# Pooled attention with an MLP behind it: one block's sum moves to TensorE, values in one group a head, and new priorities for the planner

## The chip, the cores and the metric

The kernel runs on one core of a Trainium2 chip. The metric is the device time of one launch in microseconds (us), the median of several runs. The engines of the core are TensorE (PE, its weight loads are shown as PEld), VectorE (DVE), ScalarE (ACT), GpSimd (POOL) and SyncE (SP, which only issues transfers here). Each engine works through its own queue in order.

## What is computed

Inputs are q, k, v with 4 batches, 8 heads, 1152 positions and 64 values a head, in float32. Cut to what matters:

```python
q_pool = q.reshape(B, H, S // 2, 2, D).mean(axis=3)        # 576 pooled queries
scores = scale * q_pool @ k.transpose(0, 1, 3, 2)          # 576 x 1152 a head
attn = exp(scores - max(scores))
attn = attn / (sum(attn) + 1e-9)
x = attn @ v                                               # heads side by side: 4 x 576 x 512
h = (x.transpose(0, 2, 1) @ U) @ V
u = x + h.transpose(0, 2, 1)
out = u + relu(u @ w_ch1) @ w_ch2                          # 512 -> 2048 -> 512
```

U, V, w_ch1 and w_ch2 arrive as 64-bit floats and are turned into 32-bit ones on the chip ("decode").

## The kernel before

**A head.** The 1152 keys of a head are nine blocks of 128. Queries and keys are transposed on PE, and split into a high part (rounded) and a low part. PE scans all scores once for the row maxima (lines 643 and 645, into PSUM banks of the class m); DVE reduces each scan to a maximum (line 649). Then PE makes the scores of each block with the maximum already taken off (lines 703 and 704, into banks s), and ACT writes their exponentials to SBUF (line 710). Eight of the nine blocks lie in pairs in seven tiles of a region (p2), the ninth alone in one of two tiles (p1). The sums over keys are made in two steps: an addition of 128 x 576 per block into the tile acc (line 686, seven plus the first, which joins two blocks: eight a head), on DVE or POOL, whichever the planner finds free, and then `total()` (line 721), four matmuls for a pair of heads that add acc over its partitions with a matrix of ones, each on 32 columns of PE, so that four stand side by side. The values (line 729) are matmuls of the exponentials with v, two side by side on 64 columns, into one bank that is copied out by ACT (line 737). After the odd head of a pair the outputs are transposed, divided by the sums and put into X (lines 753 to 780).

**Groups of values.** `GV` (line 267) says in which groups a head's blocks are multiplied with v: in batches 0 and 1 blocks 0 to 5 and then 6 to 8, in batches 2 and 3 all nine at once. In batches 0 and 1 (`APART`) the totals are an operation of their own; in 2 and 3 they follow in the value group of the odd head.

**A batch.** After eight heads `tail` (line 785) makes the low-rank mix and the MLP of the batch; lines 937 and 981 are the first MLP matrix, line 1028 the second. The MLP of a batch runs interleaved with the heads of the next one. The weights are decoded once (lines 409 to 426 and 861, 862, on ACT, DVE and POOL), with the MLP of the first batch, and read back by the later ones. PSUM has three banks of class s and five of class m; value groups, scans, transposes and MLP products all take m.

**What sets the order.** The program doesn't issue in the order of its loops. Each operation goes to a planner (`Plan`, from line 43) with a due time `at`, the engines it may run on, and a cost for each. The planner simulates the five queues with these costs, takes at each step the operation with the earliest due time that can start within 30 ns of the first that can, and fixes the order of every queue and the tile of every buffer. Due times are made of `T(G)`, the start of the head plus G ninths of a head's length (`HEAD0` for the first nine heads, `HEAD` later); SUM, AV, KS, QT, KT, MX0, MXS, MLP_START, MLP_RATE, DEC_START and DEC_LEAD shift single kinds of work. `a_(n)` (line 365) is the planner's cost of an ACT instruction of n elements, MOVE (130 ns) an addition to it for copies between partitions, TSW (300 ns) the planner's cost for a change of PE's column mode. The chip then runs the fixed queues in its own time.

Of the kernel before, what the change touches and what calls it, by code (L numbers as in the profile page):

```python
# [227 lines left out]
def kernel(  # L228
# [17 lines left out]
    nc = tc.nc  # L246
    B, H, S, D = q.shape
    NQ = S // 2
    DM = H * D
    DFF = moe_w_ch1.shape[1]  # L250
    R = moe_U.shape[1]
    U64, V64, W1, W2 = (w.bitcast(I32) for w in (moe_U, moe_V, moe_w_ch1, moe_w_ch2))
    P = 128
    NJ = S // P
    HALF = NQ // 2
# [3 lines left out]
    QP, NQT = 96, 6  # L259
    NG = NJ  # L260
    FG = 2
    QT, KS = -9.70, -11.74
    LEAD = 60e3, 9e3
    WHOLE_KEYS, SPLIT = (False, False, True, True), 8
    NB, QUICK = 320, (False, False, False, True)
    NARROW, NP2 = 256, 7
    GV = [((0, 6), (6, 9))] * 2 + [((0, 9),)] * 2
    TSW = 300.0
    SUM, AV, YT = 0.78, 0.73, 0.79
    NS = 6  # L270
    APART = (True, True, False, False)
    KT, MX0, MXS = 0.77, -8.58, 4.36
    V_LO = slice(2 * R, 3 * R)
    WARM_UP, WARM_N, FILL, FILL_N = 5000.0, 13, 90.0, 70
    NWHOLE = H + 1
    EXP_MIN, EXP_MAX = 2.0 ** -15, 122879.9921875
    SCALE = 0.5 / float(D) ** 0.5
    HEAD0, HEAD = 16.89e3, 21.00e3
    SLOT = HEAD / NG
    MLP_START, MLP_RATE = 4.90, (2.21, 2.21, 2.18, 2.2)  # L280
    DEC_START, DEC_LEAD = 98.0e3, 12.5e3
    SLACK = 30.0
    BIAS, BIAS_FROM = -300.0, 0.0

# [6 lines left out]
    op = plan.op  # L291
# [9 lines left out]
    ones = sb.tile([P, R], F32, name="ones")  # L301
# [7 lines left out]
    def cut(of, first, n, shape, rows=P):  # L309
# [14 lines left out]
        T1=cut(room, 0, 2, (S,)),  # L324
# [5 lines left out]
        acc=slots("acc", 3, [P, NQ]),  # L330
        ay=slots("ay", 2, [P, 2, HALF]),
# [77 lines left out]
    def decode(at, n, load, raw, t, far):  # L409


        tv = lambda: t.t[:, 0:n]
        hi = lambda: raw.t[:, 0:n, 1]
        lo = lambda: raw.t[:, 0:n, 0]
        use = [("raw", "use")]
        for f, nb in load:
            op(at - 5e3, ("sp", dma(nb), f, 0, far, BULK), use + go, [raw])
        op(at, ("act", a_(n), lambda: nc.scalar.activation(tv().bitcast(F32), hi().bitcast(F32), AF.Abs)), [raw] + use, [t])
        op(at, ("act", a_(n), lambda: nc.scalar.activation(lo(), lo().bitcast(U32), AF.Copy, scale=2.0 ** -29)), [raw] + use, [(raw, 1)])
        op(at, ("dve", v2(n), lambda: nc.vector.tensor_scalar(  # L420
            tv().bitcast(F32), tv().bitcast(F32), EXP_MAX, EXP_MIN, op0=ALU.min, op1=ALU.max)), [t], [t], port=True)
        op(at, ("dve", v2(n), lambda: nc.vector.tensor_scalar(
            tv(), tv(), 3, 0x3FFFFFFF, op0=ALU.logical_shift_left, op1=ALU.bitwise_and)), [t], [t], port=True)
        op(at, ("dve", v_(n), lambda: nc.vector.scalar_tensor_tensor(  # L424
            tv(), hi(), -0x40000000, tv(), op0=ALU.bitwise_and, op1=ALU.bitwise_or)), [t, raw] + use, [t], port=True)
        op(at, ("pool", g_(n), lambda: nc.gpsimd.tensor_tensor(tv(), tv(), lo(), op=ALU.add)), [t, (raw, 1)] + use, [t])  # L426
# [71 lines left out]
    def head(n):  # L498
# [7 lines left out]
        T1, T2, T3, Q1, Q2, qb, acc, mp = (new(c) for c in ("T1", "T2", "T3", "Q1", "Q2", "qb", "acc", "mp"))  # L506
        odd = h % 2
        if not odd:
            pair[:] = [new(c) for c in ("ay", "sr", "sm", "rs")] + [[]]
        ay, sr, sm, rs, accs = pair  # L510
        accs.append(acc)
        op(T(-17), ("sp", dma(294912), lambda: nc.sync.dma_start(
            qt.t, q[b, h].rearrange("(t p r) d -> p t (r d)", p=QP, r=2)), 0, 1500, BULK), go if n > 1 else [], [qt])
        op(T(KS - 1), dual(NQT * D, lambda e: e.tensor_tensor(
# [47 lines left out]
        def turn_whole(part, j0, j1):  # L562

            pt_ = new("m", KEEP[1])
            n2, n1 = (j1 - j0 + 1) // 2 * P, (j1 - j0) // 2 * P
            kt_blocks = range(j0, j1, 2)

            def kT():
                for i, j in enumerate(kt_blocks):
                    m = 2 if j + 1 < j1 else 1  # L570
                    nc.tensor.transpose(pt_.t[0:m * D, i * P:(i + 1) * P], kt.t[:, j:j + m].rearrange("p a d -> p (a d)"), ident)

            at = T(QT + KT * (1 + part))
            op(at, ("pe", len(kt_blocks) * TP, kT), [(kt, 0), (T1, "use")], [pt_])
            at += 0.6 * (T(1) - T(0))
            halves = (slice(0, D), slice(D, P))
            here = lambda z: T1.t[:, j0 * P:j1 * P].rearrange("p (j i) -> p j i", i=P)[:, z::2]
            there = lambda z: pt_.t[halves[z], 0:(n1 if z else n2)].rearrange("p (j i) -> p j i", i=P)
            for z, n_ in enumerate((n2, n1)):
                if n_: op(at, ("act", a_(n_, True), lambda z=z: nc.scalar.activation(here(z)[halves[z]], there(z), AF.Copy)), [pt_], [(T1, part, z)])  # L580
            for z, n_ in enumerate((n2, n1)):
                if n_: op(at, ("dve", v_(n_) + 90, lambda z=z: nc.vector.tensor_tensor(  # L582
                    here(z)[halves[1 - z]], there(z), here(z)[halves[z]].bitcast(F32), op=ALU.subtract)),
                   [pt_, (T1, part, z)], [(T1, part, 2 + z)])
            for z, n_ in enumerate((n2, n1)):
                if n_:
                    op(at + 0.8 * (T(1) - T(0)), ("act", a_(n_, True) + z * MOVE, lambda z=z: nc.scalar.activation(
                        T2.t[0:D, j0 * P:j1 * P].rearrange("p (j i) -> p j i", i=P)[:, z::2], there(z), AF.Copy)), [pt_], [(T2, part, z)])
            c0 = j0 // 2 * P
            if part == 0:  # L590
                op(at, ("act", a_(n2, True), lambda: nc.scalar.activation(T3.t[:, c0:c0 + n2], pt_.t[:, 0:n2], AF.Copy)), [pt_], [(T3, 0)])
            else:
                if n1: op(at, ("act", a_(n1, True), lambda: nc.scalar.activation(T3.t[:, c0:c0 + n1], pt_.t[:, 0:n1], AF.Copy)), [pt_], [(T3, 1)])
                for z in range(2):
                    op(at, ("act", a_(D, True) + z * MOVE, lambda z=z: nc.scalar.activation(
                        T3.t[halves[z], c0 + n1:], pt_.t[0:D, n1 + z * D:n1 + (z + 1) * D], AF.Copy)), [pt_], [(T3, 2 + z)])
            return [(T1, part, i) for i in range(4)]

# [10 lines left out]
        else:  # L609
# [13 lines left out]
            que, way = (nc.scalar, lambda f, nbytes, far: ("act", 500, f, far)) if n else (  # L623
                nc.sync, lambda f, nbytes, far: ("sp", dma(nbytes), f, 175, 800))
            for z in range(2):
                op(T(-7), ("act", a_(S // 2) + z * MOVE, lambda z=z: nc.scalar.activation(
                    T3.t[z * 64:z * 64 + 64], T1.t[0:D, z * S // 2:(z + 1) * S // 2].bitcast(F32), AF.Copy)),
                   t1[0:2] if z == 0 else t1[1:], [(T3, z)])
            op(T(-6 if n else -20), way(lambda: que.dma_start(T2.t[0:D].bitcast(F32), T1.t[0:D].bitcast(F32)), 294912, 3300), t1, [(T2, p_, z) for p_ in range(2) for z in range(2)])
# [58 lines left out]
        for j in range(NJ):  # L688
            if j % 2 == 0:
# [7 lines left out]
                for js, qa, qz, when in todo:  # L697
                    ss, nq = new("s"), qz - qa

                    def score(js=js, qa=qa, qz=qz, nq=nq, ss=ss):  # L700
# [9 lines left out]
                    op(T(when + 0.1), ("act", a_(len(js) * nq, True), lambda js=js, qa=qa, qz=qz, nq=nq, ss=ss, p=pu[j], e=js[0] % 2: nc.scalar.activation(  # L710
                        p.t[:, e:e + len(js), qa:qz], ss.t[:, 0:len(js) * nq].rearrange("p (a n) -> p a n", n=nq), AF.Exp, scale=SCALE)),
                       [ss], [(pu[j], i % 2, 1 if qa else 0) for i in js])
            if j > 0:
                add(T(j + SUM), unit(0) if j == 1 else (lambda: acc.t), unit(j), keys((0, 1)) if j == 1 else keys((j,)) + [acc])

        pa, pk = new("m"), new("m") if odd else None

        def total():
            for e, hf in ((e, hf) for hf in range(2) for e in range(2)):
                g = 32 * (2 * hf + e)  # L720
                nc.tensor.matmul(pk.t[g:g + 32, 0:HALF], ones, accs[e].t[:, hf * HALF:(hf + 1) * HALF], start=True, stop=True)  # L721

        for j0, j1 in GV[b]:
            last = j1 == NJ and odd and not APART[b]

            def value(js=range(j0, j1), last=last):
                for j in js:
                    for hf in range(2):
                        nc.tensor.matmul(pa.t[hf * D:(hf + 1) * D, 0:HALF], vt.t[:, j], pu[j].t[:, j % 2, hf * HALF:(hf + 1) * HALF],  # L729
                                         start=(j == 0), stop=(j == NJ - 1))  # L730
                if last:
                    total()

            n_ = j1 - j0 + last
            op(T(j1 - 0.5 + AV), ("pe", n_ * 4 * (HALF / 2.4 + 2.0) + TSW, value),
               [(vt, 0)] + keys(range(j0, j1)) + (accs if last else []), [pa] + ([pk] if last else []))
        op(T(NJ + AV), ("act", a_(HALF, True), lambda: nc.scalar.activation(ay.t[:, odd], pa.t[:, 0:HALF], AF.Copy)), [pa], [(ay, odd)])

        if not odd:
            return  # L740
        if APART[b]:
            op(T(NJ + AV), ("pe", 4 * (HALF / 2.4 + 2.0) + TSW, total), accs, [pk])
        op(T(NJ + AV), ("act", a_(HALF, True), lambda: nc.scalar.activation(sr.t, pk.t[:, 0:HALF], AF.Copy)), [pk], [sr])

        first = (0, P, HALF - P)
# [39 lines left out]
    def tail(b, clock):  # L785
# [29 lines left out]
                now += mm(DM)  # L815
        trow, z = new("tr"), new("xs")
        tr, ts = (lambda: trow.t), (lambda: z.t[:, 0])
        op(now, ("act", a_(DM, True), lambda: nc.scalar.activation(tr()[0:R], ptm.t[0:R], AF.Copy)), [ptm], [(trow, 0)])
        op(now, ("act", a_(DM, True), lambda: nc.scalar.activation(tr()[3 * R:4 * R], ptm.t[R:2 * R], AF.Copy)), [ptm], [(trow, 3)])
        for c in range(1, 3):  # L820
            op(now, ("sp", dma(65536), lambda c=c: nc.sync.dma_start(tr()[c * R:(c + 1) * R], tr()[0:R]), 175), [(trow, 0)], [(trow, c)])
        op(now, ("act", a_(DM), lambda: nc.scalar.activation(ts(), tr(), AF.Copy)), [(trow, c) for c in range(4)], [(z, "s")])
# [282 lines left out]
```

## Time and profile before

| | |
|---|---|
| median of 3 runs (lowest, highest) | 902.43 us (902.14, 903.07) |
| the profiled execution | 902.65 us |
| its span, first to last instruction | 900.9 us |
| PE busy | 888.8 us, 99% |
| DVE busy | 753.9 us, 84% |
| ACT busy | 521.5 us, 58% |
| POOL busy | 208.8 us, 23% |

All durations below come from the profiled execution. Its heads of the first batch lie at about 15 to 137 us, those of the second batch, with the first MLP, up to about 375, those of the third and fourth up to about 715, and the last MLP follows. The granted TensorE clock is full speed throughout. [...] PE's matmuls overlap in the records, so the time that one takes in a full queue is read from start to start, or from the chain, whose pieces don't overlap.

### The profile page before, as it was taken

What the parts mean: (1) busy time and instruction counts of PE and PEld (TensorE: products, weight loads), DVE (VectorE), ACT (ScalarE), POOL (GpSimd) and SP (SyncE); (2) the same over time, 40 slices, a digit from 0 to 9 for tenths busy, and PEclk for the clock granted to TensorE, in tenths of its full rate; (3) what the DMA queues carried; (4) which work ended last, traced back from release to release, by engine and by line L of the source; (5) the groups of instructions that cost most, each with busy time, mean ns of one, the idle gap of its engine ahead of it and who ended that gap; (6) DMA issues with size and microseconds to landing.
All of it is one profiled execution on the core that took longest, in us unless ns stands there. A gap on an engine that the chain in (4) does not pass through costs nothing.

```text
span 900.9 us, 15589 instructions
## 1 busy us (share of the span) xinstructions
PE 888.8 (99%) x5559; PEld 721.0 (80%) x5559; DVE 753.9 (84%) x1500; ACT 521.5 (58%) x1178; POOL 208.8 (23%) x217
## 2 busy tenths in 40 slices
PE   9999999999999999999999999999999999999998
PEld 8777777677777677788887887888887778899987
DVE  8999999989999899978787878787786464898885
ACT  6877889747786677655555657556564321322220
POOL 3333455535643344220001000300200000001110
PEclk9999999999999999999999999999999999999999
DMA  5243555346566454532332432323242245565422
GB/s 171 76 129 91 166 180 161 85 168 226 170 227 188 162 193 151 173 123 72 127 110 64 134 110 71 110 87 106 80 138 84 94 169 183 168 210 179 170 106 95
DMA packets 63491, 124.00 MB, mean 138 GB/s; under 512 B 5915, under 2 KB 33078, under 8 KB 63414
## 3 DMA queue, kind: packets, MB, share of 16 engines
q1 hardware_dynamic: 62214, 118.59, 40.1%
q10 hardware_dynamic: 1200, 4.42, 2.1%
q8 instruction: 44, 0.72, 0.3%
q14 instruction: 33, 0.27, 0.1%
HBM read 96.17 MB, written 21.50 MB: 131 GB/s over the span
## 4 chain that ended last, share of the span: by engine, by line
PE 76%; DVE 13%; ACT 5%; issue 3%; POOL 2%; DMA 2%; ACTq 0%; POOLq 0%; DVEq 0%; SPq 0%
PE m L1028 19%; PE m L937 13%; PE m L729 12%; PE s L703 6%; PE s L704 6%; PE m L643 6%; PE s L981 5%; DVE mp L649 4%; DVE acc L686 2%; ACT room L382 1%; ACT big L710 1%; PE m L753 1%; PE m L903 1%; PE m L645 1%; PE m L721 1%
## 5 line engine op out<-in xcount | busy, mean ns | idle before, releaser
L710 ACT ACTIVATE big<-s 128x320 f32<-128x320 f32 (+2 forms) x448 | 203.2, 480 | 123.8 <-PE s L704 119.1
L649 DVE TENSOR_REDUCE mp<-m 128x1 f32<-128x384 f32 (+1 forms) x448 | 217.6, 534 | 23.2 <-PE m L643 22.0
L1028 PE MATMUL m<-w,hh 128*128 128x512 f32 x804 | 230.0, 398 | 0.1
L937 PE MATMUL m<-rest,w 128*128 128x512 f32 (+1 forms) x768 | 189.9, 356 | 0.7 <-DVE mp L649 0.6
L703 PE MATMUL s<-room 128*128 128x256 f32 (+2 forms) x576 | 167.3, 302 | 0.3
L1028 PEld LDWEIGHTS m<-w,hh 128*128 128x128 f32 x804 | 144.8, 188 | 27.1 <-issue 2.2
L704 PE MATMUL s<-room 65*128 65x256 f32 (+2 forms) x576 | 164.8, 298 | 0.8 <-DMA room<-mr 0.7
L729 PE MATMUL m<-big,v 128*64 128x288 f32 x1152 | 150.3, 410 | 0.0
L937 PEld LDWEIGHTS m<-rest,w 128*128 128x128 f32 x768 | 132.6, 188 | 16.2 <-issue 3.1
L686 DVE TENSOR_TENSOR acc<-acc,big 128x576 f32<-128x576 f32 x163 | 126.4, 776 | 10.2 <-ACT big L710 8.0
L643 PE MATMUL m<-room 128*128 128x384 f32 x384 | 131.7, 362 | 3.2 <-DVE room L582 0.6
L686 POOL TENSOR_TENSOR acc<-acc,big 128x576 f32<-128x576 f32 x61 | 87.0, 1425 | 161.7 <-ACT big L710 79.6
L729 PEld LDWEIGHTS m<-big,v 128*64 128x64 f32 x1152 | 78.5, 137 | 57.1 <-issue 4.8
L703 PEld LDWEIGHTS s<-room 128*128 128x128 f32 x576 | 109.0, 189 | 9.8 <-issue 1.8
L704 PEld LDWEIGHTS s<-room 65*128 65x128 f32 x576 | 108.9, 189 | 7.6 <-DMA room<-mr 1.2
L643 PEld LDWEIGHTS m<-room 128*128 128x128 f32 x384 | 70.4, 188 | 25.1 <-ACT room L382 5.6
L382 ACT ACTIVATE room<-m 64x288 fp32r<-64x288 f32 (+1 forms) x173 | 72.4, 426 | 4.2 <-PE m L538 1.3
L1032 DVE TENSOR_TENSOR X<-m,X 128x512 f32<-128x512 f32 x96 | 65.6, 684 | 10.1 <-PE m L1028 9.8
L551 POOL CAST qb<-room 64x64 fp32r<-64x64 f32 x62 | 16.9, 272 | 203.5 <-DVE acc L686 132.6
L426 POOL TENSOR_TENSOR wt<-wt,rx 128x512 int32<-128x512 int32 (+2 forms) x35 | 44.7, 1279 | 73.5 <-DVE wt L424 13.4
L941 ACT ACTIVATE hh<-m 128x512 fp32r<-128x512 f32 (+1 forms) x64 | 32.9, 514 | 40.5 <-PE m L937 38.0
L943 DVE SCALAR_TENSOR_TENSOR hh<-m,hh 128x512 fp32r<-128x512 f32 (+1 forms) x64 | 37.4, 585 | 14.2 <-ACT hh L941 13.8
(129 smaller groups left out, 1058.7 us busy)
## 6 DMA issues: line engine op xcount, KB each, us to landing
w<-wc SPq DMA_DIRECT2D x96, 512.0 KB
rx<-in_moe_w_ch_dram SPq DMA_DIRECT2D x32, 512.0 KB
wc<-w SPq DMA_DIRECT2D x32, 512.0 KB
q<-in_q_dram SPq DMA_DIRECT2D x32, 288.0 KB
v<-in_v_dram SPq DMA_DIRECT2D x32, 288.0 KB
k<-in_k_dram SPq DMA_DIRECT2D x31, 288.0 KB
room<-room ACTq DMA_DIRECT2D x15, 288.0 KB
out_dram<-X SPq DMA_DIRECT2D x12, 256.0 KB
```

What stands on the lines that cost most here:

```text
L382: ways = {"act": (a_(n, True) + hold, lambda: f(lambda o, i: nc.scalar.activation(o, i, AF.Copy)))}
L643: nc.tensor.matmul(pm.t[:, 0:w], Q1.t[:, t * P - 64:t * P + 64], T1.t[:, cs_], start=True, stop=True)
L649: op(T(MX0 + 0.3 + MXS * u / 14), ("dve", v_(w), lambda c=c, t=t, w=w, pm=pm: nc.vector.reduce_max(mp.t[:, c * 5 + t:c * 5 + t + 1], pm.t[ ...
L686: op(at, dual(NQ, lambda e: e.tensor_tensor(acc.t, a(), b_(), op=ALU.add)), r, [acc])
L703: nc.tensor.matmul(o, T1.t[:, kc], Q1.t[:, qa:qz], start=True, stop=False)
L704: nc.tensor.matmul(o, T2.t[:, kc], Q2.t[:, PAD + qa:PAD + qz], start=False, stop=True)
L710: op(T(when + 0.1), ("act", a_(len(js) * nq, True), lambda js=js, qa=qa, qz=qz, nq=nq, ss=ss, p=pu[j], e=js[0] % 2: nc.scalar.activation(p ...
L729: nc.tensor.matmul(pa.t[hf * D:(hf + 1) * D, 0:HALF], vt.t[:, j], pu[j].t[:, j % 2, hf * HALF:(hf + 1) * HALF], start=(j == 0), stop=(j == ...
L937: op(now, ("pe", mm(nb), lambda c=c, i=i, a=a, bb=bb, w=w, ph=ph, sl=sl: nc.tensor.matmul(ph.t[:, 0:nb], w.t[:, a, c * P:(c + 1) * P], (ul ...
L981: nc.tensor.matmul(bank.t[:, 0:NB], left(a, c), ub.t[:, i, bb, c], start=(c == 0 and j == 0), stop=(c == 1 and j == 2))
L1028: op(now, ("pe", mm(512), lambda f=f, i=i, a=a, bb=bb, w=w, h_=h_: nc.tensor.matmul(po.t, h_.t[:, a, ns], w.t[:, bb], start=(f == fg and i ...
L1032: op(now, ("dve", v_(512), lambda: nc.vector.tensor_tensor(x(), po.t, x(), op=ALU.add)), [po], bk[t])
```

## The change

For batch 0 (`LOOSE[0]` is 1) the addition of block 8 into acc is left out. `total()` makes two parts there: first acc, then block 8's exponentials, both accumulated into the same bank, so eight matmuls instead of four for each pair of heads. It now waits for the exponentials of block 8 of both heads. For batch 1 the values of a head are one group of nine blocks. The planner's costs of a few ACT copies are raised, and the due times are set anew. No other instruction is added or taken away.

```diff
-    QT, KS = -9.70, -11.74
+    QT, KS = -9.86, -11.64
...
-    GV = [((0, 6), (6, 9))] * 2 + [((0, 9),)] * 2
+    GV = [((0, 6), (6, 9))] + [((0, 9),)] * 3
...
-    SUM, AV, YT = 0.78, 0.73, 0.79
+    SUM, AV, YT = 0.71, 0.51, 0.79
     NS = 6
+    LOOSE = (1, 0, 0, 0)
...
-    KT, MX0, MXS = 0.77, -8.58, 4.36
+    KT, MX0, MXS = 0.79, -8.77, 4.16
...
-    HEAD0, HEAD = 16.89e3, 21.00e3
+    HEAD0, HEAD = 16.77e3, 21.01e3
...
-    MLP_START, MLP_RATE = 4.90, (2.21, 2.21, 2.18, 2.2)
-    DEC_START, DEC_LEAD = 98.0e3, 12.5e3
+    MLP_START, MLP_RATE = 5.18, (2.20, 2.21, 2.18, 2.2)
+    DEC_START, DEC_LEAD = 99.4e3, 12.6e3
...
-            if j > 0:
+            if 0 < j < NJ - LOOSE[b]:
                 add(T(j + SUM), unit(0) if j == 1 else (lambda: acc.t), unit(j), keys((0, 1)) if j == 1 else keys((j,)) + [acc])
 
         pa, pk = new("m"), new("m") if odd else None
+        loose = range(NJ - LOOSE[b], NJ)
+        accs.append([lambda: acc.t] + [unit(j) for j in loose])
+        summed.extend([acc, *keys(loose)])
+        parts = 1 + LOOSE[b]
 
         def total():
-            for e, hf in ((e, hf) for hf in range(2) for e in range(2)):
-                g = 32 * (2 * hf + e)
-                nc.tensor.matmul(pk.t[g:g + 32, 0:HALF], ones, accs[e].t[:, hf * HALF:(hf + 1) * HALF], start=True, stop=True)
+            for i in range(parts):
+                for e, hf in ((e, hf) for hf in range(2) for e in range(2)):
+                    g = 32 * (2 * hf + e)
+                    nc.tensor.matmul(pk.t[g:g + 32, 0:HALF], ones, accs[e][i]()[:, hf * HALF:(hf + 1) * HALF],
+                                     start=(i == 0), stop=(i == parts - 1))
...
-            op(T(NJ + AV), ("pe", 4 * (HALF / 2.4 + 2.0) + TSW, total), accs, [pk])
+            op(T(NJ + AV), ("pe", parts * 4 * (HALF / 2.4 + 2.0) + TSW, total), summed, [pk])
```

The raised costs are 45 and 50 ns on the two ACT instructions of a decode, and MOVE on the copies of T1, T2 and T3 (the transposed keys) and of the mix's rows that lacked it.

## Rows read from the trace of the kernel before

**Rows 1.** The page: busy time of each engine, and the slices of PE, PEld and DVE

```profile
PE 888.8 (99%) x5559; PEld 721.0 (80%) x5559; DVE 753.9 (84%) x1500; ACT 521.5 (58%) x1178; POOL 208.8 (23%) x217
...
PE   9999999999999999999999999999999999999998
PEld 8777777677777677788887887888887778899987
DVE  8999999989999899978787878787786464898885
```

**Rows 2.** Busy time by stage: stretch, its length, then each engine's busy us

```profile
20.00:137.00 117.00, 115.28 (x835) 88.15 (x834) 114.45 (x249) 96.78 (x229) 45.96 (x48) 1.00 0.44 130
137.00:375.00 238.00, 233.84 (x1408) 178.71 (x1407) 221.71 (x431) 172.39 (x381) 105.62 (x91) 1.00 0.54 176
375.00:690.00 315.00, 313.87 (x2080) 261.06 (x2081) 254.41 (x506) 184.09 (x435) 37.01 (x48) 1.00 0.32 102
```

**Rows 3.** The chain that ended last, by line, 20 to 137 us

```profile
by line: PE m L729 26.6%; PE s L703 13.1%; PE m L643 12.9%; PE s L704 12.6%; DVE mp L649 6.4%; DVE acc L686 6.0%; PE m L616 3.9%; PE m L645 2.7%; ACT room L382 2.4%; issue 1.7%; PE m L753 1.7%; ACT big L710 1.7%; PE m L721 1.6%; PE m L538 1
```

**Rows 4.** The same chain, 137 to 375 us

```profile
by line: DVE mp L649 11.9%; issue 9.3%; PE m L937 8.5%; PE m L1028 7.3%; PE m L729 6.4%; DVE acc L686 4.7%; POOL acc L686 3.1%; ACT big L710 3.1%; ACT room L382 3.0%; DMA tr<-tr 3.0%; DVE wt L424 2.9%; DVE wt L420 2.7%; DVE w L862 2.6%; POO
```

**Rows 5.** The same chain, 375 to 690 us

```profile
by line: PE m L937 20.3%; PE m L1028 17.6%; PE m L729 17.2%; PE s L704 9.1%; PE s L703 8.9%; PE m L643 8.8%; PE m L571 1.9%; PE m L753 1.5%; DVE mp L649 1.4%; PE m L721 1.4%; DMA room<-mr 1.4%; PE m L903 1.3%; PE m L645 1.0%; PE m L538 0.9%
```

**Rows 6.** Line 686, 15 to 137 us: count, ns min/median/max, first and last start

```profile
L686 DVE TENSOR_TENSOR acc<-acc,big x45: 737/748/1316, 21.1 to 133.7; 128x576 f32<-128x576 f32 x45
...
L686 POOL TENSOR_TENSOR acc<-acc,big x11: 1415/1419/1425, 22.0 to 135.3; 128x576 f32<-128x576 f32 x11
...
L686 DVE TENSOR_TENSOR acc<-big x8: 690/746/759, 19.1 to 123.8; 128x576 f32<-128x576 f32 x8
```

**Rows 7.** The chain's pieces in order of time: start, us, what

```profile
67.34 3.06 PE m L729 x24
...
72.42 1.61 PE m L729 x12
...
74.88 0.62 PE m L721 x8
...
357.17 4.52 PE m L729 x36
...
368.13 0.46 PE m L937 x2
```

**Rows 8.** PE's instructions in order of time around a group of three

```profile
228.69 0.47 PE L937 MATMUL m<-rest,w 128*128 128x512 f32 x1
229.08 1.68 PE L729 MATMUL m<-big,v 128*64 128x288 f32 x12
230.69 0.39 PE L703 MATMUL s<-room 128*128 128x256 f32 x1
```

**Rows 9.** Busy time during value groups: six and three (batch 1), nine (batch 2)

```profile
221.60:224.60 3.00, 3.00 (x25) 1.63 (x24) 3.00 (x6) 1.69 (x3) 2.30 (x2) 1.00 0.50 200
...
sum 23.70, PE 23.70 PEld 12.96 DVE 23.55 ACT 11.32 POOL 11.39; mean PE 2.96 PEld 1.62 DVE 2.94 ACT 1.42 POOL 1.42
...
sum 12.00, PE 12.00 PEld 6.05 DVE 10.70 ACT 11.58 POOL 3.45; mean PE 1.50 PEld 0.76 DVE 1.34 ACT 1.45 POOL 0.43
...
357.10:361.50 4.40, 4.40 (x37) 2.50 (x36) 3.39 (x7) 3.80 (x8) 2.02 (x4) 1.00 0.36 120
...
sum 35.20, PE 35.20 PEld 19.81 DVE 20.34 ACT 23.88 POOL 3.37; mean PE 4.40 PEld 2.48 DVE 2.54 ACT 2.99 POOL 0.42
```

**Rows 10.** Who PE's weight loads waited for, 137 to 375 us: total us, times, longest

```profile
PEld m L643 <- DVE mp L649: 2.9, 11, 0.5
```

**Rows 11.** Decode on DVE, 137 to 375 us, by form: busy us, mean ns

```profile
L424 DVE SCALAR_TENSOR_TENSOR wt<-rx,wt 128x512 int32<-128x512 int32 x27 | 20.7, 766 | 0.2
L862 DVE TENSOR_TENSOR w<-wt,w 128x512 fp32r<-128x512 f32 x27 | 20.1, 746 | 1.7 <-ACT w L861 1.6
...
L420 DVE TENSOR_SCALAR wt<-wt 128x512 f32<-128x512 f32 x27 | 13.5, 500 | 1.9 <-ACT wt L418 1.8
L422 DVE TENSOR_SCALAR wt<-wt 128x512 int32<-128x512 int32 x27 | 13.5, 500 | 0.2
```

More of the change, by code (lines that the diff above doesn't have):

```diff
@@ L417, in decode @@
             op(at - 5e3, ("sp", dma(nb), f, 0, far, BULK), use + go, [raw])
-        op(at, ("act", a_(n), lambda: nc.scalar.activation(tv().bitcast(F32), hi().bitcast(F32), AF.Abs)), [raw] + use, [t])
-        op(at, ("act", a_(n), lambda: nc.scalar.activation(lo(), lo().bitcast(U32), AF.Copy, scale=2.0 ** -29)), [raw] + use, [(raw, 1)])
+        op(at, ("act", a_(n) + 45, lambda: nc.scalar.activation(tv().bitcast(F32), hi().bitcast(F32), AF.Abs)), [raw] + use, [t])
+        op(at, ("act", a_(n) + 50, lambda: nc.scalar.activation(lo(), lo().bitcast(U32), AF.Copy, scale=2.0 ** -29)), [raw] + use, [(raw, 1)])
         op(at, ("dve", v2(n), lambda: nc.vector.tensor_scalar(
@@ L508, in head @@
         if not odd:
-            pair[:] = [new(c) for c in ("ay", "sr", "sm", "rs")] + [[]]
-        ay, sr, sm, rs, accs = pair
-        accs.append(acc)
+            pair[:] = [new(c) for c in ("ay", "sr", "sm", "rs")] + [[], []]
+        ay, sr, sm, rs, accs, summed = pair
         op(T(-17), ("sp", dma(294912), lambda: nc.sync.dma_start(
@@ L579, in turn_whole @@
             for z, n_ in enumerate((n2, n1)):
-                if n_: op(at, ("act", a_(n_, True), lambda z=z: nc.scalar.activation(here(z)[halves[z]], there(z), AF.Copy)), [pt_], [(T1, part, z)])
+                if n_: op(at, ("act", a_(n_, True) + MOVE, lambda z=z: nc.scalar.activation(here(z)[halves[z]], there(z), AF.Copy)), [pt_], [(T1, part, z)])
             for z, n_ in enumerate((n2, n1)):
@@ L586, in turn_whole @@
                 if n_:
-                    op(at + 0.8 * (T(1) - T(0)), ("act", a_(n_, True) + z * MOVE, lambda z=z: nc.scalar.activation(
+                    op(at + 0.8 * (T(1) - T(0)), ("act", a_(n_, True) + MOVE, lambda z=z: nc.scalar.activation(
                         T2.t[0:D, j0 * P:j1 * P].rearrange("p (j i) -> p j i", i=P)[:, z::2], there(z), AF.Copy)), [pt_], [(T2, part, z)])
@@ L594, in turn_whole @@
                 for z in range(2):
-                    op(at, ("act", a_(D, True) + z * MOVE, lambda z=z: nc.scalar.activation(
+                    op(at, ("act", a_(D, True) + MOVE, lambda z=z: nc.scalar.activation(
                         T3.t[halves[z], c0 + n1:], pt_.t[0:D, n1 + z * D:n1 + (z + 1) * D], AF.Copy)), [pt_], [(T3, 2 + z)])
@@ L625, in head @@
             for z in range(2):
-                op(T(-7), ("act", a_(S // 2) + z * MOVE, lambda z=z: nc.scalar.activation(
+                op(T(-7), ("act", a_(S // 2) + MOVE, lambda z=z: nc.scalar.activation(
                     T3.t[z * 64:z * 64 + 64], T1.t[0:D, z * S // 2:(z + 1) * S // 2].bitcast(F32), AF.Copy)),
@@ L732, in value @@
                     total()
-            n_ = j1 - j0 + last
+            n_ = j1 - j0 + last * parts
             op(T(j1 - 0.5 + AV), ("pe", n_ * 4 * (HALF / 2.4 + 2.0) + TSW, value),
-               [(vt, 0)] + keys(range(j0, j1)) + (accs if last else []), [pa] + ([pk] if last else []))
+               [(vt, 0)] + keys(range(j0, j1)) + (summed if last else []), [pa] + ([pk] if last else []))
         op(T(NJ + AV), ("act", a_(HALF, True), lambda: nc.scalar.activation(ay.t[:, odd], pa.t[:, 0:HALF], AF.Copy)), [pa], [(ay, odd)])
@@ L817, in tail @@
         tr, ts = (lambda: trow.t), (lambda: z.t[:, 0])
-        op(now, ("act", a_(DM, True), lambda: nc.scalar.activation(tr()[0:R], ptm.t[0:R], AF.Copy)), [ptm], [(trow, 0)])
-        op(now, ("act", a_(DM, True), lambda: nc.scalar.activation(tr()[3 * R:4 * R], ptm.t[R:2 * R], AF.Copy)), [ptm], [(trow, 3)])
+        op(now, ("act", a_(DM, True) + MOVE, lambda: nc.scalar.activation(tr()[0:R], ptm.t[0:R], AF.Copy)), [ptm], [(trow, 0)])
+        op(now, ("act", a_(DM, True) + MOVE, lambda: nc.scalar.activation(tr()[3 * R:4 * R], ptm.t[R:2 * R], AF.Copy)), [ptm], [(trow, 3)])
         for c in range(1, 3):
```

## The prediction

> **What bounds the kernel now.** I read the page first: TensorE (PE) is busy for 99% of the span and VectorE (DVE) for 84%, but the slices show that DVE's share is 9 tenths almost throughout the first 16 of 40 slices and 7 to 8 after them [rows 1]. So the kernel has stages with different limits, and the second view is the busy time by stage [rows 2]. In the heads of the first batch (20 to 137 us) DVE has 114.45 of 117.00 us and PE 115.28. In the heads of the second batch with the first MLP and its weight decode (137 to 375) DVE has 221.71 of 238.00. In the third and fourth batch (375 to 690) PE has 313.87 of 315.00 and DVE only 254.41. The change puts or removes work in the first two stretches; the third gets new priorities alone.
>
> The third view is the chain that ended last, in the same stretches. In the first batch the PE lines printed hold 75% of it, VectorE's reductions and additions 12.4%, ScalarE and "issue" most of the rest [rows 3]. In the second batch no engine owns it: the three largest PE lines hold 22%, six DVE and POOL lines 27.9%, "issue" 9.3% [rows 4]. In the third and fourth the seven largest entries are all PE lines, and hold 84% [rows 5]. A microsecond saved early reaches the end, since PE is full from 375 on; a microsecond added on PE early is lost as far as PE is on the chain there.
>
> **Part 1, first batch: the last block's addition goes from DVE to PE.** Each head made eight additions of 128x576. In 15 to 137 us, 53 of the 64 ran on DVE at 748 ns and 11 on POOL at 1419 [rows 6]. The change drops one in eight: 8 x 53/64 = 6.6 DVE additions, 6.6 x 0.748 = 5.0 us of DVE (and 1.4 times 1.419, 2.0 us, of POOL, which is far from full there [rows 2]). Nothing else waited in the dropped place but the totals, so what was queued behind the additions on DVE (reductions, low parts of keys and queries) moves up.
>
> PE pays. A total is eight logged matmuls now and takes 0.62 us with its surroundings [rows 7]; four pairs of heads get eight more each. The increment alone is in the value groups: 36 logged matmuls take 4.52 us and 24 take 3.06, so twelve more cost 1.46, two at a time side by side 0.243 a step [rows 7]. The totals stand four side by side, eight make two steps, 0.49 us; I take that, since no second mode change comes with it, and 0.62 as the upper end. Four pairs: +1.95 us (to +2.5). The last block's exponentials are now held until the pair's total, but their region has two tiles and the next use of the held one is a head later: nothing.
>
> What of this reaches the time? If PE sets the stretch, +1.95. If DVE does (its idle time is 2.55 us of 117), -5.0. Both engines stand at about 98% [rows 2], so neither row is nearer, and I take the middle: (1.95 - 5.0) / 2 = **-1.5 us**.
>
> A rule speaks to this choice. The row shows PE at 98.5% matmul-busy but weight loads at only 88.15 of 117.00, 75% [rows 2]. The Trainium skill (Perfetto Trace Analysis, Identifying the Most-Contended Engine) says matmul busy time is a poor measure of PE's room and that the busy share of the weight loads should be taken; by it PE would have a quarter to spare, the 1.95 us would be hidden and part 1 would give the full -5.0. Against it: in a group of nine value blocks matmuls follow each other without a gap and the weight loads are busy for 2.48 of 4.40 us only [rows 9]. So 75% here does not prove room, and I stay with the middle.
>
> **Part 2, second batch: values in one group a head.** It removes eight groups; the matmuls stay the same. A group of six and one of three take 3.06 + 1.61 = 4.67 us, one of nine 4.52 [rows 7]: 0.15 saved. Entering costs too: before a group of three the last matmul of line 937 holds 0.39 us to the next start (228.69 to 229.08) [rows 8] where two such take 0.46 [rows 7], so 0.16 more. Per head 0.31, for eight 2.5 us of PE. That is between nothing (PE off the chain) and -2.5; the PE lines seen hold 22% of the chain there, and with the smaller ones that the row cuts off perhaps a third: -0.8. Also the output's PSUM bank, one of five, is no longer held from the first group to the end of the second, some 9 us a head (221.6 to 230.6, [rows 8, 9]). Scans that waited for a bank that a reduction had to empty are 2.9 us in this stretch [rows 10]; between 0 and -2.9, I take a tenth, -0.3, because only waits inside that hold can go. Part 2: **-1.1 us**. The exponentials of the first six blocks are held longer; batches three and four already do so on the same seven tiles, with PE idle only 1.13 us in 315 [rows 2, 9]. No DMA moves with the values: the group issues matmuls only, and their V tile was held to the second group anyway.
>
> **Part 3, counted copies and priorities.** These change the planner's costs (+45, +50 and +130 ns on some ScalarE copies) and due times (queries 0.16 slots earlier, values 0.22 slots earlier, the mix decode 1.4 us later) and so only the order on the queues: SP's loads for q, k and v keep their due times, ScalarE's own DMA of keys too. No row prices an order. In 375 to 690, where nothing else changes, PE idles 1.13 us [rows 2], so an order can give back about that; I take a loss of the same size as the other end (an estimate), and nothing as the value. The cover is PE's unbroken queue; if it is gone, a late copy shows as a gap before scans.
>
> Sum: -1.5 - 1.1 + 0 = -2.6 us. The profiled execution took 902.65 (span 900.9 and 1.75 around it), 0.22 above the median of 902.43. From the median: **899.8 us**. A measurement of this kernel can tell about 0.2%, 1.8 us, from no change.
>
> **Rivals.**
> A. *The chain decides, not the middle: no change.* PE holds at least 75% of the first batch's chain and DVE 12.4% [rows 3]. Then 0.78 x 1.95 = +1.5 and 0.13 x -5.0 = -0.65, in all +0.9; with part 2's -1.1 the sum is -0.2: 902.2 us. For it: PE is fed in order and the planner rebuilds the balance. Against it: a chain is one of several of nearly the same length, and DVE has 2% idle.
>
> B. *Slower: groups of nine starve DVE in the second batch.* Scores and scans come from PE; during a group DVE lives on what is queued. In the six-groups of this batch DVE is busy 23.55 of 23.70 us, in the three-groups 10.70 of 12.00, so it idles 0.18 us a head; in a group of nine it is idle 1.01 of 4.40 us while the decode still ran (357.1) and 1.86 on average [rows 9]. At 1.01: 0.83 us a head more, 6.6 for eight heads, in a stretch where DVE is 93% busy and PE holds about a third of the chain, so about two thirds count: +4.4. PE's saving is then hidden; with part 1's -1.5 it gives +2.9: 905.3 us. It decides from about 0.6 us of added idle a head (0.6 x 8 x 0.67 = 3.2, 1.7 net, the limit of what can be told). Against it: this batch has 67.8 us of decode on DVE that waits for no matmul [rows 11], 8 us a head.
>
> C. *DVE alone sets the first batch.* This is the rule of the weight loads as a mechanism: PE's gaps absorb the added 0.49 us a pair and the full -5.0 comes; with -1.1, 896.3 us. For it: 2.55 us of DVE idle. Against it: the full weight-load pattern above.
>
> That the change does not do what it says could be so if the dropped additions were POOL's; 11 of 64 were, which is in the sum.
>
> **How the numbers follow.** Forecast 0.42, A 0.25, B 0.18, C 0.15. Faster by over 0.2% (below 900.6): C and six sevenths of the forecast (0.36), 0.51. Slower (above 904.2): B 0.18 and, for a bad order, 0.05 of A and the forecast: 0.23. Same: 0.26. The range goes from 896.0, where C begins, to 904.8, which takes in A with order's +1.1 and the milder half of B; C's lower and B's upper part are left out, about 2 in 10. The likeliest case's own range is 898 to 901.5.
>
> **What would show it.** Right: 56 additions instead of 64 in the first batch's heads, totals of 16 logged matmuls at about 1.1 us, the first batch's last value group some 1.5 us sooner; in the second batch eight groups of 36 and about 2 us less between its first and last. DVE's busy time down by about 5 us, PE's idle time not up. Wrong: the first batch ends no sooner and the chain there has more PE (A); DVE idle over 0.6 us in each group of nine of the second batch, with additions or decode on the chain behind it (B); DVE still at 98% of a first batch that is 4 us shorter (C). If the third and fourth batch change length by over 1 us, part 3 was not nothing.

## The result and the profile after

The changed kernel takes 894.38 us (median of 6 runs, 892.72 to 895.65) against 902.49 for the one before on the same chips: a ratio of 0.991 with a 95% interval of 0.9901 to 0.992. The forecast was 899.8, and its range began at 896.0. The sign was right, the size was not: 8.1 us instead of 2.6.

The page after, as in [rows 1] (the profiled execution took 894.45 us, its span is 892.7):

```profile
PE 883.3 (99%) x5591; PEld 724.2 (81%) x5591; DVE 742.0 (83%) x1480; ACT 525.4 (59%) x1184; POOL 220.5 (25%) x223
...
DVE  7999999989999899788788888787786464898885
```

The busy time by stage of the changed kernel, to be held against [rows 2]; the second and third stretch begin and end earlier here:

```profile
20.00:137.00 117.00, 116.05 (x868) 89.41 (x868) 112.22 (x246) 99.78 (x234) 47.37 (x50) 1.00 0.46 136
137.00:367.00 230.00, 227.05 (x1417) 180.10 (x1416) 215.54 (x423) 175.46 (x386) 106.84 (x88) 1.00 0.55 178
367.00:682.00 315.00, 314.71 (x2087) 262.19 (x2087) 252.32 (x501) 183.60 (x434) 45.08 (x54) 1.00 0.33 102
```

PE's share grows in each, and DVE is busy for 12 us less in all. Some 9 of the 12 are additions: DVE made 190 of the 256 before and makes 178 of 248 now, so the planner also moved four to POOL. (Each value and total matmul stands twice in the trace: nine blocks in two halves are 18 matmuls and 36 records.) Where the time came from is read best from the last value group of a head. PE's instructions in order of time (start, length, engine), heads 0, 7, 10, 16, 24 and 31, of the kernel before:

```profile
28.25 1.68 PE L729 MATMUL m<-big,v 128*64 128x288 f32 x12
133.01 1.68 PE L729 MATMUL m<-big,v 128*64 128x288 f32 x12
205.81 1.68 PE L729 MATMUL m<-big,v 128*64 128x288 f32 x12
357.10 4.59 PE L729 MATMUL m<-big,v 128*64 128x288 f32 x36
549.18 4.59 PE L729 MATMUL m<-big,v 128*64 128x288 f32 x36
713.95 4.59 PE L729 MATMUL m<-big,v 128*64 128x288 f32 x36
```

and of the changed kernel, where line 729 is line 735 and head 10 has one group:

```profile
30.00 1.68 PE L735 MATMUL m<-big,v 128*64 128x288 f32 x12
134.09 1.68 PE L735 MATMUL m<-big,v 128*64 128x288 f32 x12
201.78 4.59 PE L735 MATMUL m<-big,v 128*64 128x288 f32 x36
348.23 4.59 PE L735 MATMUL m<-big,v 128*64 128x288 f32 x36
542.93 4.59 PE L735 MATMUL m<-big,v 128*64 128x288 f32 x36
705.91 4.59 PE L735 MATMUL m<-big,v 128*64 128x288 f32 x36
```

From end to end of these groups (start plus length), the stretches are 104.8, 72.8, 154.2, 192.1 and 164.8 us before, and 104.1, 70.6, 146.5, 194.7 and 163.0 after. So heads 0 to 7, in which the additions were dropped, gain 0.7; heads 7 to 10 gain 2.2; heads 10 to 16 gain 7.7; heads 16 to 24, whose matmuls are the same, lose 2.6, and 24 to 31 gain 1.8. The start, 1.75 us later after, is no part of the change (last section). In what follows these stretches are given for every kernel, worked out in the same way from its profile.

### The profile page after: what moved, and what is told of

It is laid out like the page before. It is cut to its first block, busy times and chain, and to the rows that moved or that the text cites. A ratio compares the mean times of both kernels' runs of the same rounds, so it can differ in the third digit from the quotient of the medians.

```text
span 892.7 us, 15618 instructions
## 1 busy us (share of the span) xinstructions
PE 883.3 (99%) x5591; PEld 724.2 (81%) x5591; DVE 742.0 (83%) x1480; ACT 525.4 (59%) x1184; POOL 220.5 (25%) x223
## 4 chain that ended last, share of the span: by engine, by line
PE 61%; DVE 6%; ACT 1%; issue 1%; DMA 0%; DVEq 0%
PE m L1034 19%; PE m L943 12%; PE m L735 8%; PE s L987 6%; PE s L704 4%; PE s L703 4%; PE m L643 4%; DVE mp L649 1%; PE m L571 1%; DVE acc L686 1%; PE m L909 1%; PE m L759 1%; PE m L818 1%; PE m L726 1%; DVE X L1038 1%
## 5 line engine op out<-in xcount | busy, mean ns | idle before, releaser
L943 PE MATMUL m<-rest,w 128*128 128x512 f32 (+1 forms) x768 | 184.6, 354 | 0.0
L703 PE MATMUL s<-room 128*128 128x256 f32 (+2 forms) x576 | 169.1, 304 | 1.9 <-ACT big L710 1.6
L735 PE MATMUL m<-big,v 128*64 128x288 f32 x1152 | 148.5, 410 | 0.0
L686 POOL TENSOR_TENSOR acc<-acc,big 128x576 f32<-128x576 f32 x66 | 94.2, 1428 | 150.5 <-ACT big L710 81.1
L686 DVE TENSOR_TENSOR acc<-acc,big 128x576 f32<-128x576 f32 x150 | 120.3, 802 | 13.1 <-ACT big L710 10.2
L643 PE MATMUL m<-room 128*128 128x384 f32 x384 | 129.3, 360 | 0.4 <-DVE mp L649 0.3
```

Source lines behind the costliest of these rows:

```text
L643: nc.tensor.matmul(pm.t[:, 0:w], Q1.t[:, t * P - 64:t * P + 64], T1.t[:, cs_], start=True, stop=True)
L686: op(at, dual(NQ, lambda e: e.tensor_tensor(acc.t, a(), b_(), op=ALU.add)), r, [acc])
L703: nc.tensor.matmul(o, T1.t[:, kc], Q1.t[:, qa:qz], start=True, stop=False)
L943: op(now, ("pe", mm(nb), lambda c=c, i=i, a=a, bb=bb, w=w, ph=ph, sl=sl: nc.tensor.matmul(ph.t[:, 0:nb], w.t[:, a, c * P:(c + 1) * P], (ul ...
```

## The experiments

**Each part alone, and each left out.** Call the groups of the second batch G, the sum on PE L, the counted copies C and the due times D. The edits are the hunks of the diff above. `only_` kernels have one of them, `all_but_` kernels all but one.

```diff
# only_groups: the kernel before with
+    GV = [((0, 6), (6, 9))] + [((0, 9),)] * 3
# only_loose: the kernel before with LOOSE = (1, 0, 0, 0) and the code that reads it
# only_costs: the kernel before with + MOVE, + 45, + 50
# only_due: the kernel before with QT to DEC_LEAD as changed
# all_but_loose: the changed kernel with
-    LOOSE = (1, 0, 0, 0)
+    LOOSE = (0, 0, 0, 0)
# all_but_groups, all_but_costs, all_but_due: in the same way
```

> The kernel before with one edit: the second batch's values in one group a head. After the change the first nine heads end 1 to 2 us later than before and the whole gain, 11 us, comes between head 9 and head 16. Theory G (the groups do it: eight mode changes less and the output's PSUM bank freed for scans): 895 to 898 us, and heads 9 to 16 gain 5 us or more. Theory O (the new order, due times and counted copies, does it): 901 to 903. Theory L (the additions dropped in the first batch let the decode run ahead): 901 to 903.

> The kernel before with one edit: the first batch's last block is summed on TensorE. Theory L: 895 to 898 us, decode operations of the first MLP 10 us or more earlier, and the gain shows behind head 9. Theory G and theory O: 901 to 904, since TensorE gets 1.95 us more work in the first batch. My recorded forecast for this part alone was -1.5 us, 901.0.

> The kernel before with one edit: the planner's costs of the ScalarE copies raised as in the change. No instruction is added or removed, only the order changes. Theory O: 2 us or more faster, 897 to 900. Theories G and L: within 1.8 us of 902.5.

> The kernel before with one edit: all due times as in the change. Only the order changes. Theory O: 2 us or more faster, 897 to 900. Theories G and L: within 1.8 us of 902.5, or slower, since the times were set for other work.

Measured: only_groups 901.88 us (ratio 0.9983, 0.9973 to 0.9994), only_loose 904.0 (1.0019), only_costs 909.64 (1.0074), only_due 906.03 (1.0035). None of the theories stands as it was put: three of the four parts alone make the kernel slower, and the fourth gives 0.5 us. Half of theory G came all the same: in the profile of only_groups heads 10 to 16 take 146.6 us, 7.6 less than before and as long as in the changed kernel. (That execution took 899.14 us, the shortest of its ten.)

> The changed kernel with the second batch's values back in groups of six and three, all else as changed. Theory G: the gain goes, 899 us or more. Theories O and L: 894 to 897, at most the eight mode changes' 2.5 us are lost.

> The changed kernel with the first batch's last addition back in acc and the totals in one part. Theory L: the gain goes, 899 us or more. Theories G and O: 892 to 895, as TensorE is rid of 1.95 us.

> The changed kernel with the planner's costs of ScalarE copies as before. Theory O: 896 to 900. Theories G and L: within 1.8 us of 894.4.

> The changed kernel with all due times as before. Theory O: 897 to 902. Theories G and L: 894 to 897.

Measured: 898.7, 900.97, 902.37 and 901.18 us. Every part left out costs 4 to 8 us, also those that cost time alone. The parts don't add up; what one is worth depends on which others are there.

**The parts without the order, and the order without the parts.**

```diff
# both_parts: the changed kernel with C and D undone (G and L stay)
# order_only: the changed kernel with G and L undone (C and D stay)
```

> The changed kernel with costs and due times as before: the last block's sum on TensorE and the groups of nine, in the old order's priorities. Theory S (each part has a value of its own and the values add): 902.4 - 0.5 + 1.7 = 903.6 us, 902.5 to 904.7. Theory I (the parts need an order that was set for them): 902 to 908, not below 901. Theory N (any small change of the order moves the time by several us, whatever it is for): anywhere from 897 to 909.

> The changed kernel with the first batch's additions and the second batch's groups as before: new costs and due times on the old work. Theory S: 902.4 + 7.3 + 3.7 = 913 us. Theory I: 904 to 910, slower than before, since the due times were set for the other work. Theory N: anywhere from 897 to 909.

Measured: both_parts 898.02 us (ratio 0.9956, 0.9941 to 0.9971), order_only 900.71 (0.9978). Theory S misses both, by 5.6 and 12 us; I said slower for the order and it is faster. With C and D taken as one switch (order), eight kernels are complete:

| | two groups | one group (G) |
|---|---|---|
| old order | 902.4 | 901.9 |
| old order, L | 904.0 | 898.0 |
| new order | 900.7 | 901.0 |
| new order, L | 898.7 | 894.4 |

Over the four pairs that differ in it alone, G is worth -0.5, -6.0, +0.3 and -4.3, on average -2.6; L +1.6, -3.9, -2.0 and -6.6, on average -2.7; the order -1.7, -5.3, -0.9 and -3.6, on average -2.9. The three averages make up the 8.1, but the single pairs spread by 4 to 8 us, and by the medians G gives something only where L is there.

**The same pairs by stage, and the clock.** The stretches of the profiled executions say more. In each cell the first kernel has two groups in the second batch and the second has one, all else alike:

| | heads 0 to 7 | 7 to 10 | 10 to 24 |
|---|---|---|---|
| old order: before, only_groups | 104.8, 104.9 | 72.8, 74.5 | 346.3, 341.2 |
| old order, L: only_loose, both_parts | 105.6, 105.8 | 71.8, 71.7 | 345.9, 341.4 |
| new order: order_only, all_but_loose | 109.7, 108.6 | 70.6, 71.4 | 344.1, 343.0 |
| new order, L: all_but_groups, changed | 104.1, 104.1 | 71.1, 70.6 | 344.6, 341.2 |

Heads 10 to 24 gain by G in all four, also without L: 5.1, 4.5, 1.1 and 3.4 us. Heads 0 to 7, where G changes nothing, depend on L and the order together: L makes them 0.8 to 1.0 longer in the old order and 4.5 to 5.6 shorter in the new one. Those 5 us lie in head 7 alone (in all 20 profiles heads 0 to 6 take 89.6 to 91.7). In head 7 PE stops once for over 1 us, in all_but_loose before

```profile
133.85 0.38 PE L704 MATMUL s<-room 65*128 65x256 f32 x1 [1.18 <-DMA room<-mr]
```

and order_only, all_but_costs and all_but_due stop there too, for 1.2 to 1.6 us; the last two have L, so the stop comes and goes with the order and not with the sum's own work. After such stops the granted clock can fall. In all_but_loose, and in only_groups at another place (stretch, its length, busy us of PE, PEld, DVE, ACT and POOL, then the granted clock):

```profile
134.20:137.60 3.40, 3.40 (x13) 2.09 (x13) 3.32 (x8) 3.31 (x8) 2.56 (x3) 0.50 0.09 23
```

```profile
164.50:167.90 3.40, 3.03 (x13) 1.56 (x15) 3.29 (x7) 3.25 (x9) 1.09 (x1) 0.50 0.55 124
```

Half of full speed is 1.2 GHz, for 3.4 us, so up to 1.7 us are lost (an estimate: PE then does half its work). all_but_loose has a second such stretch at 164.9 us; order_only (135.5), all_but_due (135.7) and only_costs (392.6) have one, only_due two (175.2 and 376.6), groups_all below one of 6.8 us. PE had stood still for 0.8 to 1.7 us in all just before each; in all_but_costs it did so for 1.3 us and the clock stayed full. The kernels before and changed, both_parts, only_loose and all_but_groups have none. So both cells of the first table in which G seems to give nothing carry this loss: only_groups up to 1.7 us of it, all_but_loose up to 3.4, order_only up to 1.7. The executions that weren't profiled fit: the mean granted clock is under 0.999 in all ten of only_groups and of all_but_loose, and in one of the 50 of the kernel before beside them.

**How far an order alone moves the time.** Due times moved by a hundredth of a slot reorder the queues in places: in before_nudge_keys and after_nudge_mlp all five, but in after_nudge_keys only five places of PE's, so that kernel is all but the changed one over again.

```diff
# after_nudge_keys (before_nudge_keys: 0.77 to 0.78)
-    KT, MX0, MXS = 0.79, -8.77, 4.16
+    KT, MX0, MXS = 0.80, -8.77, 4.16
# after_nudge_mlp
-    MLP_START, MLP_RATE = 5.18, (2.20, 2.21, 2.18, 2.2)
+    MLP_START, MLP_RATE = 5.19, (2.20, 2.21, 2.18, 2.2)
```

> The changed kernel with one due time moved by a hundredth of a slot (the key transposes, KT 0.79 to 0.80, some 20 ns): a change that means nothing by itself. Theories S and I: 893 to 896.5 us, as the changed kernel. Theory N: 3 us or more slower, 897 to 905.

> The kernel before with the same due time moved by a hundredth of a slot (KT 0.77 to 0.78). Theories S and I: 901 to 904 us, as the kernel before. Theory N: 3 us or more away from it, most likely slower, 905 to 910.

> The changed kernel with the MLP's start moved by a hundredth of a slot (5.18 to 5.19, 23 ns): all five queues are reordered in places, no work changes. If the gain belongs to the work: 893 to 897. If it is a lucky order: 897 to 903.

Measured: 894.4, 901.59 and 897.53 us. The nudges of the keys change under 1 us, after_nudge_keys having hardly moved anything; the nudge of the MLP costs 3.1, as was said of a lucky order: some 3 of the 8.1 us may be no more than that. In its profile heads 10 and 16 start their groups at

```profile
200.76 4.59 PE L735 MATMUL m<-big,v 128*64 128x288 f32 x36
...
353.78 4.59 PE L735 MATMUL m<-big,v 128*64 128x288 f32 x36
```

153.0 us apart where the changed kernel has 146.5, with the same work in the same groups; heads 16 to 24 give 2.8 back (191.9 against 194.7). A stretch of a sixth of the kernel can differ by 6 us through the order (where the queues agree, in after_nudge_keys and in sum_left_out below, each of these stretches repeats within 0.5), and a sum over two stretches is steadier than each.

**The groups, by that sum.** From head 10 to head 24 nine kernels with one group in the second batch (among them both nudges of the changed kernel and groups_all below) take 339.4 to 344.9 us, on average 342.1; seven with two groups as before take 343.7 to 349.7, on average 346.2. The two longest of the seven, only_costs and only_due, have 3.4 us at half clock there; without them the average is 344.9. So the groups are worth some 3 to 4 us there (3.5 in the mean of the four pairs), with orders spreading by 3 us to either side.

Why more than the mode changes? The output's bank is held from its first write to the end of its copy by ACT. One head of the kernel before:

```profile
221.63 3.13 PE L729 MATMUL m<-big,v 128*64 128x288 f32 x24
...
229.08 1.68 PE L729 MATMUL m<-big,v 128*64 128x288 f32 x12
...
231.71 0.39 ACT L737 ACTIVATE ay<-m 128x288 f32<-128x288 f32 x1
```

and of the changed one:

```profile
226.60 4.59 PE L735 MATMUL m<-big,v 128*64 128x288 f32 x36
...
231.24 0.41 ACT L743 ACTIVATE ay<-m 128x288 f32<-128x288 f32 x1 [1.02 <-PE m L735]
```

10.5 us and 5.0; over the eight heads of the second batch 87.2 us and 43.1. Two kernels take hold and mode changes apart:

```diff
# hold_bank: the changed kernel with
+        if b == 1:
+            op(T(6 - 0.5 + AV), ("pe", FILL, lambda: nc.tensor.transpose(pa.t[:, 0:P].bitcast(F32R), identr, identr)), keys(range(0, 6)), [pa])
         for j0, j1 in GV[b]:
# late_split: the changed kernel with GV as before, and
-            op(T(j1 - 0.5 + AV), ("pe", n_ * 4 * (HALF / 2.4 + 2.0) + TSW, value),
+            op(T((8.4 if b == 1 and j1 == 6 else j1) - 0.5 + AV), ("pe", n_ * 4 * (HALF / 2.4 + 2.0) + TSW, value),
```

> The changed kernel; in the second batch a small transpose (53 ns of TensorE) writes the output's bank where the group of six used to stand, so the bank is taken as early as before the change, and the values stay one group. Theory B (the bank's hold was the cost): most of the gain of heads 10 to 16 goes, the stretch is back at 150 us or more, 898 us or more in all. Theory M (the mode changes and TensorE's unbroken queue): within 1.5 us of 894.4.

> The changed kernel with the second batch's values in groups of six and three, the group of six due 0.6 slots before the group of three instead of 3 slots: both mode changes, but the bank is held for a shorter time. Theory B: near the changed kernel with the eight mode changes' 2.5 us more at most, 894.5 to 897. Theory M: like the kernel with the groups undone, 898 to 900.

Measured: hold_bank 900.95 us (ratio 0.9979, 0.9967 to 0.9991), late_split 897.44 (0.9934, 0.9913 to 0.9955). In hold_bank's trace the small transpose takes the bank and the values follow 5 us later:

```profile
220.81 0.23 PE L730 MATMUL m<-identr 128*128 128x128 f32 x1
226.01 4.59 PE L737 MATMUL m<-big,v 128*64 128x288 f32 x36
```

With the bank held for 79.0 us in all and no second mode change, heads 10 to 24 take 347.8 us, 6.7 more than the changed kernel and more than any of the nine. With both mode changes but 61.0 us of hold they take 343.7, 2.5 more, within the nine kernels' spread. hold_bank fits theory B and not theory M, though 2.8 of its 6.7 us lie in heads 16 to 24, where it changes no work. late_split decides nothing: its time lies between the two forecasts, 0.4 us above B's and 0.6 below M's, and its 343.7 between the changed kernel's 341.2 and the 344.6 of all_but_groups. Each is one order, and orders move this stretch by 3 us either way, so the bank's hold is a likely cause and not a shown one.

**Whether the added sum costs PE anything.** The second part of the totals is left out, so the first batch's sums lack the last block; DVE's, ACT's, POOL's and SP's queues are the same, and PE's lack only these matmuls.

```diff
# sum_left_out: the changed kernel with
-            for i in range(parts):
+            for i in range(1):
...
-                                     start=(i == 0), stop=(i == parts - 1))
+                                     start=(i == 0), stop=True)
```

> The changed kernel without the second part of the first batch's totals, so the last block's exponentials are missing from the sums there; every queue keeps its order. If TensorE sets the first batch, as half of my forecast had it: 1.95 us faster, 892 to 893. If VectorE sets it: 894 to 895, no change.

Measured: 892.46 us, 1.9 below the changed kernel, as if TensorE set the first batch; the stretches say otherwise. Heads 0 and 7:

```profile
28.39 1.68 PE L735 MATMUL m<-big,v 128*64 128x288 f32 x12
...
132.53 1.68 PE L735 MATMUL m<-big,v 128*64 128x288 f32 x12
```

104.1 us apart, as in the changed kernel, although three of the four pairs' sums (1.5 us of PE) are gone. In this order they are hidden in the first batch. Heads 7 to 10, with the last pair's, are 0.7 shorter, 10 to 24 0.6. The profiled executions differ by 2.8, of which 1.6 is the start; so the sum costs about 1 us. In the old order L makes heads 0 to 7 longer, by 0.8 and 1.0 us in the table by stage, so there the sum may not be hidden.

What the dropped additions gave is seen in DVE's time on additions (line 686) between 20 and 137 us, before and then after

```profile
20.00:137.00 117.00, 39.54 (x52) 1.00 0.44 130
```

```profile
20.00:137.00 117.00, 35.57 (x46) 1.00 0.46 136
```

4.0 us less. From head 0 to head 7 it is 4.1 us less of additions and 2.3 us more of the MLP's decode (lines 420 to 424 of the kernel before, on DVE: 10.3 us before, 12.6 after), so DVE used more than half of it to work ahead, and the heads got hardly shorter. Heads 7 to 10, with 3.3 us less decode (line 862 counted), did. only_loose shows the same without the new order: 4.9 us less of additions and 3.0 more of decode in heads 0 to 7, and heads 7 to 10 shorter by 1.0.

**More of the same.**

```diff
# loose_both: the changed kernel with
-    LOOSE = (1, 0, 0, 0)
+    LOOSE = (1, 1, 0, 0)
# groups_all: the changed kernel with
-    GV = [((0, 6), (6, 9))] + [((0, 9),)] * 3
+    GV = [((0, 9),)] * 4
```

> The changed kernel with the last block summed on TensorE in the second batch too, due times as they are. If VectorE's relief counts where its decode runs: 2 us or more faster, 890 to 892. If TensorE sets the second batch now: 1.95 us slower, 896 to 897. If the order it falls into decides: anything from 893 to 900.

> The changed kernel with one group of nine in the first batch too, so in all batches. Theory B (the bank's hold costs wherever scans want banks): heads 0 to 7 shorter than 104.1 us by 1 to 3, 891.5 to 893.5 in all. If VectorE alone sets the first batch: heads 0 to 7 within 1 us of 104.1, or longer since VectorE lives on what TensorE hands it and is at 97% there; 894 to 900.

Measured: loose_both 900.01 us, groups_all 907.56. The first costs 5.7 us from head 10 to 24, three times what PE's added work explains, so the order has its part. The second lengthens heads 0 to 7 from 104.1 to 114.5. Who waited for whom there (30 to 140 us: us, times, longest), in groups_all

```profile
ACT big L710 <- PE s L704: 14.0, 24, 2.7
```

and in the changed kernel

```profile
ACT big L710 <- PE s L704: 4.2, 14, 0.8
```

ScalarE, busy for 92.87 of 107 us from 30 to 137 in the changed kernel, goes without scores for longer, and falls to 86.55. But that accounts for little of the 10.4 us: heads 0 to 6, in which 11.7 of the 14.0 us of waiting lie, lengthen by 0.9 us only (91.1 from 90.2), and head 7 alone by 9.5 (23.4 from 13.9). There PE stops for 1.6 us at 133 us, and then has half the clock (1.2 GHz) for 6.8 us, up to 3.4 us lost:

```profile
134.50:141.30 6.80, 6.49 (x24) 5.06 (x26) 6.23 (x13) 5.80 (x13) 2.44 (x3) 0.50 0.52 130
```

It is a stop like that of order_only and the others; what the groups of nine have to do with it is not shown. No version here that computes the reference beats the changed kernel.

## Why the prediction was wrong

**Part 3 failed first.** "Nothing as the value", with an order's reach put at 1.1 us from PE's idle time in the third and fourth batch. The new costs and due times were worth -0.9 to -5.3 us in the four pairs, -3.6 with both other parts in place, and their halves alone +7.3 and +3.7. Two things were wrong in that price. It was read in 375 to 690 us and used for the whole kernel: from both_parts to the changed kernel, which differ in the order alone, heads 0 to 7 shorten by 1.7 us, 7 to 10 by 1.1 and 24 to 31 by 1.0. And PE's idle row doesn't bound what waits cost: in heads 10 to 24 hold_bank has five small transposes more than the changed kernel, and PE is logged busy for 343.7 us instead of 339.6, so a part of its waiting stands in the records as busy time. That an order can also bring a stretch at half clock was in no row of the kernel before.

**Part 2 was mis-sized.** Its work was right: eight groups of 36, entering and leaving saved. Its price was not. I took a third of 2.5 us since PE held a third of the chain, and a tenth of 2.9 for the bank; the stretch from head 10 to 24 alone, with five of the eight groups, got 3 to 4 us. The chain names one path; in a stage where five engines change places on it, a third of a saving is no bound. The bank's term was made small by its waits in the row of [rows 10], which counts only the waits of scans that a reduction ended, and the hold was 87.2 us over the eight heads, 10.9 a head and not 9. hold_bank's 6.7 us suggests that this was the larger term; how the 3 to 4 us divide between bank and mode changes stays open.

**Part 1 was right in its pieces and wrong in its place.** The totals take two steps more. In the changed kernel:

```profile
106.40 0.69 PE L726 MATMUL m<-acc,ones 128*32 128x288 f32 x8
106.91 0.67 PE L726 MATMUL m<-big,ones 128*32 128x288 f32 x8
107.50 0.62 PE L643 MATMUL m<-room 128*128 128x384 f32 x2
```

1.10 us from first to next, where the chain had 0.62 [rows 7]: 0.48 more, 0.49 was forecast. DVE's relief was 4.0 us, 5.0 forecast. But heads 0 to 7 became 0.7 us shorter, not 1.5, and the middle between "PE sets" and "DVE sets" describes neither: in the new order PE's addition was hidden (sum_left_out), DVE's relief went in large part into decode, and what L gained there (4.5 to 5.6 us by the table) came in head 7, which goes without its stop then; the sum had no such term.

The Trainium skill (Perfetto Trace Analysis, Identifying the Most-Contended Engine) tells not to take PE's room from matmul busy time. This trace agrees: in the new order PE was logged busy for 116.05 of 117.00 us, 1.5 us of added work among them, without a longer stretch. My objection, that a group of nine has idle weight loads in a full queue, was true and did not bear on it.

**The rivals.** A (no change) is out. B, the starved DVE, did not come: the eight groups of nine of the second batch, summed,

```profile
sum 35.20, PE 35.20 PEld 19.72 DVE 32.44 ACT 28.76 POOL 16.79; mean PE 4.40 PEld 2.47 DVE 4.05 ACT 3.60 POOL 2.10
```

leave DVE idle for 2.76 us, 0.35 a head, against [rows 9]'s 0.18 and the 0.6 from which it would decide: the decode filled them, as was said against it. In groups_all ScalarE waits longer for scores, at a cost of 0.9 us in heads 0 to 6. C came nearest in time (896.3) with half its mechanism: the sum is hidden in the new order, but the heads did not shorten by DVE's relief.

What stays open: why PE stops in head 7 in the kernels that have the costs and due times without L, or L with only one of the two, and how much of G's gain is the bank. That G seems to give nothing without L is in large part the clock and head 7, as the table by stage shows; due times set anew for G alone were not tried.

## What to carry to other kernels

Where a planner fixes the queues, a change of one part is a change of every queue: price the parts from rows, but give the order a range from nudges that mean nothing (0.7 and 3.1 us here, and see first that a nudge does reorder the queues), and test parts in pairs under both orders, not one by one. Compare stage by stage, and read the granted clock of every profile first: a stop of PE of about 1 us can cost up to 1.7 us more through the clock (the estimate above). Count how long an accumulating PSUM bank is held, not only who is seen waiting for it. Relief on a full engine shows where that engine's work was waiting, which may be a stage later.

## What the runs showed of the hardware

The start of a launch is not repeatable to a microsecond: the changed kernel and sum_left_out, whose queues are alike up to the first total, have their first head's last group at 30.00 and at 28.39 us. PE's pace shows where the difference comes from. The same matmul of line 643 and the one behind it, in the changed kernel

```profile
7.46 0.65 PE L643 MATMUL m<-room 128*128 128x384 f32 x1
7.91 0.54 PE L479 MATMUL s<-identr 128*128 128x128 f32 x3
```

and in sum_left_out

```profile
6.94 0.41 PE L643 MATMUL m<-room 128*128 128x384 f32 x1
7.19 0.38 PE L479 MATMUL s<-identr 128*128 128x128 f32 x3
```

are 0.45 and 0.25 us apart; the changed kernel has 0.26 from 10.02 us on. In six of the 20 profiles (changed, hold_bank, loose_both, before_nudge_keys, only_costs, only_loose) PE keeps the slow pace until 10 to 13 us, and head 0 ends at 31.7 to 33.1 us; in the other fourteen the fast pace is there by 7.2 us, and head 0 ends at 29.8 to 30.5. The clock column reads 1.00 in both, so here it doesn't show the pace. Two profiles are compared from a common point in the work, not from the first instruction.

In seven of the 20 profiles PE's granted clock falls to half, 1.2 GHz, for 3.4 or 6.8 us in the middle of the work, each time after PE has stood still for 0.8 to 1.7 us in all; a stop of 1.3 us in all_but_costs has no fall after it.
